# Attention scores: a mask added by two half-size products, and one reciprocal for two groups

## The chip, the cores and the metric

The kernel runs on one core of a Trainium2 chip. The metric is the device time of one execution in microseconds (us). Before the change the median of 3 runs is 858.65 us (858.62 to 858.83). The engines are PE (TensorE, matmuls; its weight loads are listed as PEld), DVE (VectorE), ACT (ScalarE), POOL (GpSimd) and SP, which issues the DMAs. Each engine runs its own instructions in program order and waits on semaphores for the others.

## What is computed

Attention with two kinds of heads, then two feed-forward blocks. 4 batches, 8 heads, 576 positions, 64 columns per head:

```python
scores = scale * np.matmul(q, k.transpose(0, 1, 3, 2))
rel = pos[:, None] - pos[None, :]
mask_local = (rel >= 0) & (rel < stride)                       # heads 0 to 3, stride = 32
mask_strided = (rel >= 0) & (pos[None, :] % stride == pos[:, None] % stride)   # heads 4 to 7
scores = np.where(masks[None, :, :, :], scores, -1000000000.0)
attn = np.exp(scores - max); attn = attn / (sum + 1e-09)
x = np.matmul(attn, v)            # 2304 rows of 512
h = x @ w_in; x = (h * np.cos(h)) @ w_out          # 512 -> 2048 -> 512
x = (silu(x @ w_gate) * (x @ w_val)) @ w_out2      # 512 -> 1536 -> 512
```

## The kernel before

The change lies in the attention stage, which takes about the first 100 us. The feed-forward stages follow it and fill the rest. All five engines' orders are those in which the code is written: there is no scheduler, and the pools only hand out buffers.

**Groups.** A unit is a pair of heads in one batch, its two heads on partitions 0 to 63 and 64 to 127. Units are strided and local in turn. Each unit is cut into 3 groups: a local group has 3 tiles of 64 queries by 96 keys, a strided one 4 tiles (the last of a unit 3) of 54 queries by 54 keys. The list `gs` holds 48 groups, strided and local alternating: even group numbers are strided, odd ones local.

**The loop.** One iteration `k` starts group `k` and carries older groups on (`LAGS` = 2, 5, 6, 7): `sums` of group k-2 (DVE: row sums, L490), `transposes` of group k-5 (PE, L501 local, L505 strided, into `tp`), `scores` of group k (PE, L466 to L469), `top` of group k (DVE: row maxima out of PSUM, L474; POOL: times the scale, L475, into `mx`), `put` of group k-7 (ACT: results to `xy`, L536, L545), `evac` of group k-5 (ACT: `tp` to `pt` or `pts`, L512), `values` of group k-6 (PE, L523, into `po`), `exps` of group k-1 (ACT, L481, bias `mx`), then `pump`, and last `norm` of group k-2 (DVE: reciprocal, L493; POOL: product, L495). So in an iteration's DVE order the reciprocal of group k-2 stands behind the pumped work, and in POOL's order the `mx` of a group and the product of an older one alternate.

**Pump.** From iteration 8 on, `pump(1.05)` takes about 1.05 us of DVE work out of a queue `fill`: the conversion of the w_in weights (ACT L254, DVE L257, L261, L265, the tile `wi`), scales (L126 to L145), the split of weights and inputs in a high and a low half (ACT L275, DVE L278), and the scan of w_out (L204). What a pump takes is fixed by the program.

**Scores.** For each tile of a group and each head, a product of 64 rows and 64 columns of the array (L466: head 0 on rows and columns 0 to 63, head 1 on 64 to 127), f32. Then a product of ones over columns 288 to 511 of the bank, whose result nobody reads (L468, bf16, the whole array), and then the identity times the mask over the whole array (L469, bf16), which adds the mask to the scores of both heads. All go to one PSUM bank: `start=True` is on the first score product.

After the 48 groups, 8 iterations drain the pipeline; in them PE does `keep_warm` products (L811) and the first tile of the feed-forward (`up1`, L581 to L583, with `up1_a`, ACT L614).

Of the kernel before, what the change touches and what calls it, by code (L numbers as in the profile page):

```python
# [10 lines left out]
F32 = mybir.dt.float32  # L11
# [39 lines left out]
LAGS = (2, 5, 6, 7)  # L51
# [30 lines left out]
def build(tc, qk_l, qk_s, v_l, v_s, w_in, w_out, w_gate, w_val, w_out2, fixed, out):  # L82
    nc = tc.nc
    wide = w_in.dtype != F32
    with ExitStack() as ctx:
# [12 lines left out]
        id16 = small.tile([128, 128], BF16, name="id16")  # L98
        ones16 = small.tile([128, 128], BF16, name="ones16")
# [75 lines left out]
        def release():  # L175
            if held_back[0]:
                held_back[0] -= 1
                next_raw()
            else:
                hold[0] = False  # L180
# [39 lines left out]
        def pump(share):  # L220

            credit[0] = min(credit[0] + share, max(share, 1.0))
            while fill and credit[0] > 0:
                step_fill()

        def need(key):
            while key not in emitted:
                step_fill()
# [99 lines left out]
        def direct_later(mat, j, tiles):  # L328
# [8 lines left out]
            rests.append((0.7, lambda: lo_part(tiles[j][:, 1], box["c"], scale_w[mat][0], tiles[j][:, 0]), (mat, j)))  # L337

        def seven_steps(j, stage, sums):

            boxes, conv = [], []
# [5 lines left out]
            def sources():  # L347
                f0, f1 = boxes[0]["c"], boxes[1]["c"]
                return ((stage[:, 0:1], f0[:, 0:256].rearrange("p (q n) -> p q n", q=1)),
                        (stage[:, 1:3], f1.rearrange("p (q n) -> p q n", q=2)), (stage[:, 3:7], sums))  # L350
# [54 lines left out]
        ap = attn.enter_context(tc.tile_pool(name="attn", bufs=2, side="right"))  # L405
# [8 lines left out]
        hot = ap.tile([128, 512], BF16, name="hot", bufs=1)  # L414
# [13 lines left out]
        def load_qk(i):  # L428
            b, p = units[i]
            loc = is_local(p)  # L430
            qk_t[i] = ap.tile([128, QKW[loc]], F32, name="qkl" if loc else "qks", bufs=3)
            nc.sync.dma_start(out=qk_t[i], in_=(qk_l if loc else qk_s)[b, p % 2])

        def load_v(i):
            b, p = units[i]
            loc = is_local(p)
            if loc:
                v_t[i] = ap.tile([128, LT, 128], F32, name="vl")
                nc.sync.dma_start(out=v_t[i], in_=v_l[b, p % 2])
            else:  # L440
                v_t[i] = v_pair[i // 2 % 2]
                for u in range(2):
                    nc.sync.dma_start(out=v_t[i][u:128:2, SP * u:SP * u + SP, :], in_=v_s[b, p % 2, u])

        def bank():
            return pm.tile([128, 512], F32, name="bank")

        class Group:
# [7 lines left out]
            def scores(self):  # L456
                n, w = self.n, self.w
                b = bank()
                self.sc = b[:, 0:n * w].rearrange("p (n w) -> p n w", w=w)
                mask = (ml[:, 0:3] if self.g == 0 else ml[:, 1:4]) if self.loc else ms[:, 0:n]  # L460
                for i in range(n):
                    q0 = (64 if self.loc else SW) * (self.i0 + i)
                    k0 = (S if self.loc else QP) + q0
                    for h in range(2):
                        r = slice(64 * h, 64 * h + 64)
                        nc.tensor.matmul(out=self.sc[r, i, :], lhsT=qk_t[self.i][r, q0:q0 + 64], rhs=qk_t[self.i][r, k0:k0 + w],  # L466
                                         start=i == 0, stop=False)
                nc.tensor.matmul(out=b[:, 288:512], lhsT=ones16, rhs=hot[:, 0:224], start=False, stop=False)  # L468
                nc.tensor.matmul(out=self.sc, lhsT=id16, rhs=mask, start=False, stop=True)  # L469

            def top(self):
                self.mx = ap.tile([128, 4], F32, name="mx", bufs=3)
# [7 lines left out]
                    e = self.t[:, i, 0:self.w] if self.loc else self.t[:, i // 2, 0:self.w, i % 2]  # L480
                    nc.scalar.activation(out=e, in_=self.sc[:, i, :], func=AF.Exp, scale=SCALE, bias=self.mx[:, i:i + 1])  # L481

            def sums(self):

                self.ls = ap.tile([128, 4], F32, name="ls", bufs=5)
                if self.loc:
                    self.l, self.e = self.ls[:, 0:3], self.t
                else:
                    self.l, self.e = self.ls.rearrange("p (a u) -> p a u", u=2), self.t.rearrange("p a k u -> p a u k")
                nc.vector.tensor_reduce(out=self.l, in_=self.e[..., 0:self.w + 1], op=ALU.add, axis=AX.X)  # L490

            def norm(self):
                nc.vector.reciprocal(out=self.l, in_=self.l)  # L493
                e = self.e[..., 0:self.w]
                nc.gpsimd.tensor_tensor(out=e, in0=e, in1=self.l.unsqueeze(len(e.shape) - 1).to_broadcast(list(e.shape)), op=ALU.mult)  # L495

# [104 lines left out]
        def up1(blk, m, ks=range(KC), c=None, spare=None):  # L601
            n = BLOCKS[blk][1]
            if m == 0 and not c:
                turn[blk] = prod(sx[blk][1], scale_w["in"][1], 1.0 / TWO_PI)
            if not c:
                b = bank() if spare is None else pacc.tile([128, 512], F32, name=f"acc{spare}")
                c = dict(n=n, ph=b[:, 0:n], blk=blk)
            project(c["ph"], wi[m], xs[blk], n, ks)
            return c

        def up1_a(c):
            n = c["n"]
            c["w"] = ring.tile([128, 512], F32, name="tb", bufs=4)[:, 0:n]
            nc.scalar.activation(out=c["w"].bitcast(I32), in_=c["ph"], func=AF.Identity, scale=turn[c["blk"]], bias=quarter)  # L614
# [194 lines left out]
        def keep_warm():  # L809
            t = bank()[:, 0:4 * LW].rearrange("p (n w) -> p n w", w=LW)  # L810
            nc.tensor.matmul(out=t, lhsT=id16, rhs=ml, start=True, stop=True)  # L811

        for k in range(len(gs) + LAGS[3] + 1):
            def group(lag):
                return gs[k - lag] if 0 <= k - lag < len(gs) else None
            i, g = 2 * (k // 6), k % 6
            if group(LAGS[0]):
                group(LAGS[0]).sums()
            if group(LAGS[1]):
                group(LAGS[1]).transposes()  # L820
            if group(0):
                group(0).scores()
                group(0).top()
            begun = k - len(gs) - K0
            if 0 <= begun < 2 * EARLY:
                m = begun // 2
                if begun % 2 == 0:
                    need(("in", m))
                    early = up1(0, m, range(KC // 2))
                else:  # L830
                    up1(0, m, range(KC // 2, KC), early)
                    up1_a(early)
                    steps.append((0, m, early))
            elif not group(0):
                keep_warm()
            if group(LAGS[3]):
                group(LAGS[3]).put()
            if group(LAGS[1]):
                group(LAGS[1]).evac()
            if group(LAGS[2]):  # L840
                group(LAGS[2]).values()
            if group(0) and g == 5:
                for j in (i + 2, i + 3):
                    if i and j < len(units):
                        load_v(j)
                for j in (i + 6, i + 7):
                    if j < len(units):
                        load_qk(j)
            if group(1):
                group(1).exps()  # L850
            pump(PUMP if k >= KP else 0)
            if group(LAGS[0]):
                group(LAGS[0]).norm()
            if k >= RELEASE:
                release()

# [344 lines left out]
        for s, (blk, j) in enumerate(slots):  # L1201
            n = BLOCKS[blk][1]
            h = n // 2
# [18 lines left out]
            def snap(src, h=h):  # L1222
                t = halves(ring.tile([128, 512], F32, name="cv", bufs=3), h)
                nc.scalar.activation(out=t, in_=src, func=AF.Copy)  # L1224
                return t
# [7 lines left out]
            a = begun or snap(px)  # L1233
# [7 lines left out]
            b = snap(pz)  # L1241
# [6 lines left out]
            a = snap(px)  # L1248
# [116 lines left out]
```

## Time and profile before

The profiled execution took 859.65 us; its span, first to last instruction, is 858.0 us.

| engine | busy us | share of span | instructions |
|---|---|---|---|
| PE | 844.9 | 98% | 7223 |
| PEld | 601.9 | 70% | 7223 |
| DVE | 653.6 | 76% | 1256 |
| ACT | 520.4 | 61% | 1047 |
| POOL | 200.0 | 23% | 281 |

How to read it: the shares are averages over stages with different limits, so a stage is read by the stretches of the table by windows. The granted TensorE clock is 1.00 of full speed throughout. A PE record's length contains the pipeline's latency, so what a PE instruction costs is the distance from its start to the next one's start. DVE and ACT records overlap their neighbours a little in the same way. In the chain that ended last, PE has 83%, DVE 11%.

### The profile page before, as it was taken

Reading aid. Unit: us, or ns where it says so; the run is one execution under the profiler, and the core shown is the slowest. Engines: PE = TensorE matmul, PEld = TensorE weight load, DVE = VectorE, ACT = ScalarE, POOL = GpSimd, SP = SyncE. Lnnn points to the kernel's source line nnn. Section 1 sums busy time; section 2 is a strip of 40 time slices with the busy share of each in tenths; the row PEclk is TensorE's granted clock in tenths of the full one; section 3 lists DMA queues with packets and bytes.
Section 4 is the critical chain, followed back from the end, with each engine's and each line's share of the span. In section 5 each row is a group of like instructions: output and inputs, shape, how many; then the busy total and the mean of one; then the engine's idle time right before and its main releaser. Section 6 shows DMA issues by size and latency. Waiting matters only on the chain.

```text
span 858.0 us, 18338 instructions
## 1 busy us (share of the span) xinstructions
PE 844.9 (98%) x7223; PEld 601.9 (70%) x7223; DVE 653.6 (76%) x1256; ACT 520.4 (61%) x1047; POOL 200.0 (23%) x281
## 2 busy tenths in 40 slices
PE   9999999999999999999999999999999999999998
PEld 5777544444444444555666788888888899999998
DVE  6999989997888978789996378567756765765562
ACT  6899889554657766768885466545344444444440
POOL 3454234211445546423223100000000000000000
PEclk9999999999999999999999999999999999999999
DMA  9998822897567566514356257667777688789894
GB/s 364 408 381 274 280 90 78 282 337 260 167 198 240 198 214 205 178 34 177 131 193 249 75 194 282 230 218 263 235 262 239 238 273 289 280 306 319 323 321 145
DMA packets 53605, 202.21 MB, mean 236 GB/s; under 512 B 5264, under 2 KB 15888, under 8 KB 49680
## 3 DMA queue, kind: packets, MB, share of 16 engines
q1 hardware_dynamic: 53520, 201.06, 67.3%
q8 instruction: 56, 0.92, 0.4%
q14 instruction: 29, 0.24, 0.1%
HBM read 177.05 MB, written 23.99 MB: 234 GB/s over the span
## 4 chain that ended last, share of the span: by engine, by line
PE 83%; DVE 11%; DMA 2%; ACT 2%; issue 1%; POOL 0%; SPq 0%; ACTq 0%; POOLq 0%
PE acc L734 14%; PE bank L581 13%; PE bank L582 12%; PE bank L583 12%; PE acc L583 7%; PE acc L581 7%; PE acc L582 7%; PE bank L466 3%; PE po L523 2%; DMA raw<-w_val 2%; DVE tb L624 1%; DVE tb L617 1%; PE tp L501 1%; DVE cv L265 1%; PE bank L468 1%
## 5 line engine op out<-in xcount | busy, mean ns | idle before, releaser
L581 PE MATMUL bank<-xs,wi 128*128 128x256 f16 (+3 forms) x776 | 231.1, 298 | 4.4 <-DVE q L145 1.7
L583 PE MATMUL bank<-xs,wi 128*128 128x256 f16 (+3 forms) x776 | 231.1, 298 | 0.0
L582 PE MATMUL bank<-xs,wi 128*128 128x256 f16 (+3 forms) x776 | 231.1, 298 | 0.0
L629 POOL TENSOR_TENSOR arena<-tb,arena 128x512 f16<-128x512 f32 (+1 forms) x80 | 91.5, 1144 | 239.6 <-ACT arena L628 212.9
L582 PEld LDWEIGHTS <-wi 128*128 128x128 f16 x880 | 86.1, 98 | 41.5 <-issue 7.2
L583 PE MATMUL acc<-arena 128*128 128x512 f16 (+1 forms) x320 | 114.5, 358 | 0.5 <-DVE arena L278 0.5
L581 PE MATMUL acc<-arena 128*128 128x512 f16 (+1 forms) x320 | 114.5, 358 | 0.0
L582 PE MATMUL acc<-arena 128*128 128x512 f16 (+1 forms) x320 | 114.5, 358 | 0.0
L581 PEld LDWEIGHTS <-wi 128*128 128x128 f16 x880 | 86.1, 98 | 36.0 <-issue 1.1
L583 PEld LDWEIGHTS <-wi 128*128 128x128 f16 x880 | 86.1, 98 | 34.7
L734 PEld LDWEIGHTS <-arena 128*128 128x128 f16 x1080 | 100.7, 98 | 8.1
L719 POOL TENSOR_TENSOR wi<-tb 128x256 f32<-128x256 f32 (+1 forms) x30 | 20.2, 675 | 338.5 <-DVE tb L701 338.5
L704 ACT ACTIVATE arena<-tb 128x256 f16<-128x256 f32 (+3 forms) x59 | 28.6, 485 | 99.0 <-DVE tb L701 90.6
L1228 DVE TENSOR_TENSOR arena<-bank,cv 128x512 f32<-128x512 f32 (+1 forms) x60 | 37.9, 636 | 66.0 <-PE bank L583 66.0
L583 PEld LDWEIGHTS <-arena 128*128 128x128 f16 x600 | 58.7, 98 | 33.7 <-DVE arena L278 1.0
L734 PE MATMUL acc<-arena 128*128 128x256 f16 (+1 forms) x702 | 82.0, 265 | 0.0
L582 PEld LDWEIGHTS <-arena 128*128 128x128 f16 x600 | 58.7, 98 | 32.6
L581 PEld LDWEIGHTS <-arena 128*128 128x128 f16 x600 | 58.7, 98 | 32.4
L628 ACT ACTIVATE arena<-tb 128x512 f16<-128x512 f32 (+1 forms) x80 | 46.6, 583 | 53.5 <-PE acc L583 51.9
L614 ACT ACTIVATE tb<-bank,quarter,c 128x512 int32<-128x512 f32 (+1 forms) x74 | 53.7, 725 | 33.7 <-PE bank L583 25.5
L701 DVE SCALAR_TENSOR_TENSOR tb<-tb,c,arena 128x512 f32<-128x512 f32 (+1 forms) x60 | 41.7, 695 | 35.8 <-ACT tb L696 35.8
L1224 ACT ACTIVATE cv<-bank 128x512 f32<-128x512 f32 (+1 forms) x90 | 49.3, 548 | 30.1 <-PE bank L583 29.1
(143 smaller groups left out, 1722.3 us busy)
## 6 DMA issues: line engine op xcount, KB each, us to landing
wi<-w SPq DMA_DIRECT2D x20, 1792.0 KB, 7.7
arena<-w SPq DMA_DIRECT2D x60, 576.0 KB, 4.9
raw<-w_out SPq DMA_DIRECT2D x56, 512.0 KB, 4.7
arena<-w SPq DMA_DIRECT2D x10, 1792.0 KB, 8.9
raw<-w_gate SPq DMA_DIRECT2D x24, 512.0 KB, 4.2
raw<-w_val SPq DMA_DIRECT2D x24, 512.0 KB, 5.6
w<-arena SPq DMA_DIRECT2D x42, 256.0 KB, 3.0
raw<-w_in SPq DMA_DIRECT2D x16, 512.0 KB, 9.1
```

The costliest lines, as they stand in the source:

```text
L466: nc.tensor.matmul(out=self.sc[r, i, :], lhsT=qk_t[self.i][r, q0:q0 + 64], rhs=qk_t[self.i][r, k0:k0 + w], start=i == 0, stop=False)
L581: nc.tensor.matmul(out=o, lhsT=w[:, 0, c], rhs=x[0], start=first, stop=False, **kw)
L582: nc.tensor.matmul(out=o, lhsT=w[:, 0, c], rhs=x[1], start=False, stop=False, **kw)
L583: nc.tensor.matmul(out=o, lhsT=w[:, 1, c], rhs=x[0], start=False, stop=last, **kw)
L614: nc.scalar.activation(out=c["w"].bitcast(I32), in_=c["ph"], func=AF.Identity, scale=turn[c["blk"]], bias=quarter)
L628: nc.scalar.activation(out=g[:, 0, 0:n], in_=w, func=AF.Copy)
L629: nc.gpsimd.tensor_tensor(out=g[:, 1, 0:n], in0=w, in1=g[:, 0, 0:n], op=ALU.subtract)
L701: nc.vector.scalar_tensor_tensor(out=t, in0=t, scalar=s_g[c["blk"]], in1=c["C"][m][:, 1, 0:c["n"]], op0=ALU.mult, op1=ALU.mult)
L704: nc.scalar.activation(out=to, in_=src, func=AF.Copy, scale=2.0 ** -11)
L734: nc.tensor.matmul(out=o[:, c], lhsT=w[:, 256 * i + 128 * c:256 * i + 128 * c + 128], rhs=unit(u)[:, x:x + h], start=j == c == i == 0, sto ...
L1224: nc.scalar.activation(out=t, in_=src, func=AF.Copy)
L1228: nc.vector.tensor_tensor(out=c["C"][m][:, :, h * right:h * right + h], in0=p, in1=t, op=ALU.add)
```

## The change

Three edits. First, the product of ones moves ahead of the score products and takes `start=True`. Second, the mask is added by two products of 64 rows and 64 columns, one a head, on the same quarters of the array as the scores. Third, the sums of a strided group and of the local group behind it go to one tile `ls` of 8 columns, and one reciprocal of 7 columns serves both: `sums` of the local group, then `invert`, then both `norm` products, all at the head of the local group's iteration; the strided group's norm thereby moves from the end of one iteration to the head of the next, the local group's from the end to the head of the same iteration.

```diff
@@ scores
                 mask = (ml[:, 0:3] if self.g == 0 else ml[:, 1:4]) if self.loc else ms[:, 0:n]
+                nc.tensor.matmul(out=b[:, 288:512], lhsT=ones16, rhs=hot[:, 0:224], start=True, stop=False)
                 for i in range(n):
...
                         nc.tensor.matmul(out=self.sc[r, i, :], lhsT=qk_t[self.i][r, q0:q0 + 64], rhs=qk_t[self.i][r, k0:k0 + w],
-                                         start=i == 0, stop=False)
-                nc.tensor.matmul(out=b[:, 288:512], lhsT=ones16, rhs=hot[:, 0:224], start=False, stop=False)
-                nc.tensor.matmul(out=self.sc, lhsT=id16, rhs=mask, start=False, stop=True)
+                                         start=False, stop=False)
+                for h in range(2):
+                    r = slice(64 * h, 64 * h + 64)
+                    nc.tensor.matmul(out=self.sc[r], lhsT=id16[r, r], rhs=mask[r], start=False, stop=True)
@@ sums, norm
-            def sums(self):
-                self.ls = ap.tile([128, 4], F32, name="ls", bufs=5)
+            def sums(self, mate):
                 if self.loc:
-                    self.l, self.e = self.ls[:, 0:3], self.t
+                    self.ls = mate.ls
+                    self.l, self.e = self.ls[:, 4:7], self.t
                 else:
...
+                    self.ls = ap.tile([128, 8], F32, name="ls", bufs=3)
+                    self.l = self.ls[:, 0:4].rearrange("p (a u) -> p a u", u=2)
...
+            def invert(self):
+                nc.vector.reciprocal(out=self.ls[:, 0:7], in_=self.ls[:, 0:7])
             def norm(self):
-                nc.vector.reciprocal(out=self.l, in_=self.l)
@@ the loop
             if group(LAGS[0]):
-                group(LAGS[0]).sums()
+                mate = group(LAGS[0] + 1)
+                group(LAGS[0]).sums(mate)
+                if group(LAGS[0]).loc:
+                    mate.invert()
+                    mate.norm()
+                    group(LAGS[0]).norm()
...
             pump(PUMP if k >= KP else 0)
-            if group(LAGS[0]):
-                group(LAGS[0]).norm()
```

On PE, one strided group before (`ones_77` are the weights of ones, `id_76` the identity, `fix` the mask's tile):

```order
L501 MATMUL tp<-fix,e_l_103 96x128 x3
L466 MATMUL bank<-qks 64x54 x8
L468 LDWEIGHTS ones_77
L468 MATMUL bank<-hot,ones_77 128x224
L469 LDWEIGHTS id_76
L469 MATMUL bank<-fix,id_76 128x216
L523 MATMUL po<-pts,v_pair_108 64x54 x8
```

and the same group now:

```order
L507 MATMUL tp<-fix,e_l_103 96x128 x3
L461 LDWEIGHTS ones_77
L461 MATMUL bank<-hot,ones_77 128x224
L467 MATMUL bank<-qks 64x54 x8
L471 LDWEIGHTS id_76
L471 MATMUL bank<-fix,id_76 64x216
L471 LDWEIGHTS id_76
L471 MATMUL bank<-fix,id_76 64x216
L529 MATMUL po<-pts,v_pair_108 64x54 x8
```

The whole-array product of ones now follows the whole-array transposes, and the mask follows the scores on the same quarters; a group has one matmul and one weight load more.

On POOL, where `e_s` and `e_l` are the exponentials of strided and local groups, a piece of the loop before:

```order
L495 TENSOR_TENSOR e_s_99<-e_s_99,ls 128x2x2x54
L475 TENSOR_SCALAR mx<-mx 128x3
L495 TENSOR_TENSOR e_l_103<-e_l_103,ls 128x3x96
L475 TENSOR_SCALAR mx<-mx 128x4
L495 TENSOR_TENSOR e_s_100<-e_s_100,ls 128x2x2x54
```

and the same piece now:

```order
L501 TENSOR_TENSOR e_s_99<-e_s_99,ls 128x2x2x54
L501 TENSOR_TENSOR e_l_103<-e_l_103,ls 128x3x96
L477 TENSOR_SCALAR mx<-mx 128x3
L477 TENSOR_SCALAR mx<-mx 128x4
L501 TENSOR_TENSOR e_s_100<-e_s_100,ls 128x2x2x54
```

The `mx` of each local group (the row with 3 columns) now stands behind two products, where it stood behind one that belonged to an older iteration. The orders of ACT and SP are unchanged.

## Rows read from the trace of the kernel before

**Rows 1.** Busy us by window: instruction counts, granted clock, DMA share, GB/s.

```profile
core 0: us, PE busy (x) PEld busy (x) DVE busy (x) ACT busy (x) POOL busy (x), PEclk, DMA share, GB/s
20.00:50.00 30.00, 30.00 (x507) 21.62 (x504) 28.82 (x78) 27.32 (x105) 15.14 (x32) 1.00 1.03 408
50.00:100.00 50.00, 49.54 (x794) 34.81 (x793) 47.32 (x134) 47.02 (x172) 23.34 (x49) 1.00 0.87 296
58.00:71.50 13.50, 13.50 (x235) 9.79 (x231) 12.49 (x37) 13.50 (x49) 7.31 (x15) 1.00 0.90 332
79.10:95.40 16.30, 16.23 (x247) 11.30 (x247) 15.62 (x41) 16.30 (x58) 7.87 (x16) 1.00 0.86 273
122.00:200.00 78.00, 76.90 (x358) 34.81 (x357) 76.81 (x135) 52.81 (x84) 21.12 (x19) 1.00 0.67 230
216.00:858.00 642.00, 634.15 (x5177) 483.14 (x5176) 459.74 (x825) 355.76 (x608) 125.05 (x137) 1.00 0.65 223
```

**Rows 2.** Timeline of PE, one strided group: start us, us, instruction, count.

```profile
38.72 0.53 PE L501 MATMUL tp<-fix,e_l 128*96 128x128 f32 x3
39.18 0.67 PE L466 MATMUL bank<-qks 64*64 64x54 f32 x16
39.79 0.27 PE L468 MATMUL bank<-hot,ones 128*128 128x224 bf16 x1
39.89 0.26 PE L469 MATMUL bank<-fix,id 128*128 128x216 bf16 x1
40.09 0.68 PE L523 MATMUL po<-pts,v_pair 108*64 108x54 f32 x16
40.69 0.44 PE L505 MATMUL tp<-fix,e_s 128*128 128x128 f32 x2
41.06 0.71 PE L466 MATMUL bank<-qkl 64*64 64x96 f32 x12
```

**Rows 3.** Timeline of PE, transposes ahead of a whole-array bf16 product.

```profile
90.89 0.53 PE L501 MATMUL tp<-fix,e_l 128*96 128x128 f32 x3
91.26 0.33 PE L811 MATMUL bank<-fix,id 128*128 128x384 bf16 x1
```

**Rows 4.** Groups of instructions, 0 to 225 us: busy us, mean ns, idle before.

```profile
L493 DVE RECIPROCAL ls<-ls 128x4 f32<-128x4 f32 (+1 forms) x48 | 8.0, 167 | 0.0
```

**Rows 5.** Timeline of DVE at two places: start us, us, instruction, idle before.

```profile
66.24 0.75 DVE L278 SCALAR_TENSOR_TENSOR xs<-xy,s,xs 128x512 f16<-128x512 f32 x1 [0.57 <-ACT xs L275]
...
76.36 0.17 DVE L493 RECIPROCAL ls<-ls 128x4 f32<-128x4 f32 x1
76.45 0.42 DVE L490 TENSOR_REDUCE ls<-e_l 128x3 f32<-128x291 f32 x1
76.79 0.45 DVE L474 TENSOR_REDUCE mx<-bank 128x3 f32<-128x288 f32 x1
```

**Rows 6.** Timeline of POOL, 76 to 79 us.

```profile
76.70 0.55 POOL L495 TENSOR_TENSOR e_s<-e_s,ls 128x216 f32<-128x216 f32 x1 [1.68 <-PE tp L501]
77.32 0.20 POOL L475 TENSOR_SCALAR mx<-mx 128x3 f32<-128x3 f32 x1
78.06 0.67 POOL L495 TENSOR_TENSOR e_l<-e_l,ls 128x288 f32<-128x288 f32 x1 [0.54 <-DVE ls L493]
78.69 0.20 POOL L475 TENSOR_SCALAR mx<-mx 128x3 f32<-128x3 f32 x1
```

**Rows 7.** Timeline of ACT at three places.

```profile
38.70 0.68 ACT L254 ACTIVATE wi<-raw 128x512 f32<-128x512 f32 x1 [1.98 <-DMA raw<-w_in]
...
77.56 0.81 ACT L481 ACTIVATE e_l<-bank,mx 128x96 f32<-128x96 f32 x3 [0.41 <-POOL mx L475]
79.03 1.33 ACT L275 ACTIVATE wi<-wi,s 128x512 f16<-128x512 f32 x2 [0.67 <-DVE s L120]
80.27 0.40 ACT L545 ACTIVATE xy<-po 128x96 f32<-128x96 f32 x2
80.49 0.39 ACT L512 ACTIVATE pts<-tp 128x256 f32<-128x256 f32 x1
...
96.15 0.78 ACT L614 ACTIVATE tb<-bank,quarter,c 128x512 int32<-128x512 f32 x1 [0.70 <-PE bank L583]
```

**Rows 8.** Timeline of PE at 81 us, the product that reads `pts`.

```profile
80.95 0.68 PE L523 MATMUL po<-pts,v_pair 108*64 108x54 f32 x16
```

More of the change, by code (lines that the diff above doesn't have):

```diff
@@ L481, in exps @@
                     nc.scalar.activation(out=e, in_=self.sc[:, i, :], func=AF.Exp, scale=SCALE, bias=self.mx[:, i:i + 1])
-            def sums(self):
-                self.ls = ap.tile([128, 4], F32, name="ls", bufs=5)
+            def sums(self, mate):
                 if self.loc:
-                    self.l, self.e = self.ls[:, 0:3], self.t
-                else:
-                    self.l, self.e = self.ls.rearrange("p (a u) -> p a u", u=2), self.t.rearrange("p a k u -> p a u k")
+                    self.ls = mate.ls
+                    self.l, self.e = self.ls[:, 4:7], self.t
+                else:
+                    self.ls = ap.tile([128, 8], F32, name="ls", bufs=3)
+                    self.l = self.ls[:, 0:4].rearrange("p (a u) -> p a u", u=2)
+                    self.e = self.t.rearrange("p a k u -> p a u k")
                 nc.vector.tensor_reduce(out=self.l, in_=self.e[..., 0:self.w + 1], op=ALU.add, axis=AX.X)
+            def invert(self):
+                nc.vector.reciprocal(out=self.ls[:, 0:7], in_=self.ls[:, 0:7])
             def norm(self):
-                nc.vector.reciprocal(out=self.l, in_=self.l)
                 e = self.e[..., 0:self.w]
```

## The prediction

> **What bounds the kernel now.** I read the busy time by window first. From 216 us to the end PE is busy 634.15 of 642 us: whatever ends earlier before that, the end moves with it. From 122 to 200 us DVE is full (76.81 of 78), but its work is started by the attention stage's end and nothing there hangs on a clock of its own, so a shift passes through that too. What has to be known is how far the attention stage's end, at about 101 us, moves. There three engines stand close together: from 50 to 100 us PE is busy 49.54, DVE 47.32, ACT 47.02 of 50 us, and ACT is full from 58 to 71.5 and from 79.1 to 95.4 [rows 1].
>
> Then the timelines. PE goes through its groups without a stall, about 1.9 us each (39.18 to 41.06 is 1.88) [rows 2], so the stage looks bound by PE. But its partners follow closely. At 80.49 ACT moves `pts` out, done at 80.88, and PE starts on it at 80.95 [rows 7, 8]: 0.07 us of room. The DMA engines are full from 20 to 50 us (share 1.03) and ACT waits 1.98 us for a piece of w_in that lands at 38.70 [rows 1, 7]; that landing does not move when PE is faster. So the stage is paced by PE, with ACT less than 0.1 us behind it at some places.
>
> **PE.** What one change between whole-array and quarter-array products costs can be read: three transposes take 0.46 us up to the first quarter product (38.72 to 39.18) and 0.37 us up to a whole-array product (90.89 to 91.26), so 0.09 us [rows 2, 3]. The mask, 216 columns, takes 0.20 us up to the next form of product, the ones, 224 columns, 0.10 us up to the mask that has their own form: 0.10 us again [rows 2]. Before, a group has four such changes (into the scores, out to the ones, into the values, out to the transposes); now the ones follow the transposes and the mask the scores, and three are left. If the two mask halves run beside each other, as long as one, a group gets 0.09 us shorter: 48 x 0.09 = 4.3 us of PE. Do they? No row shows two bf16 halves. The nearest is the score block: 16 passes of 54 columns go from 39.18 to 39.79, 0.52 us without the change of form; at the transposes' pace (0.37 / 3 for 128 columns, 0.052 for 54) they would take 0.83 us one after the other [rows 2, 3]. So halves of this kind overlap, into one bank, and I take 0. Serial, they would add the columns once more, about 0.10 us. Between -0.09 and +0.01 a group I take -0.09. The extra weight load stands behind score passes and is costed at nothing; if it isn't covered, it eats at most the gain.
>
> The Trainium skill, TensorEngine Tiling (Array Packing), Restrictions and Gotchas, says the opposite of the overlap: different row tiles cannot access the same PSUM bank simultaneously. By that rule the halves would be serial and PE's sum would be +0.5 us instead of -4.3; the score rows speak against it here, where the halves write different partitions, and it stays as a rival below.
>
> **DVE.** 24 of 48 reciprocals go (those left have 7 columns instead of 3 or 4). From one's start to the next start is 0.09 us (76.36 to 76.45) [rows 5], so 24 x 0.09 = 2.2 us; the records' own 167 ns [rows 4] would be 4.0, which is the bound. Nothing else on DVE changes in number.
>
> **POOL, and what stands behind it.** The same 48 products and 48 `mx`, in another order. This is the added wait: `mx` of a local group is queued behind both products, which wait for the reciprocal. Take the group at 76 to 78 us. Sums start at 76.45, and 0.34 us later DVE is free for the reciprocal, 76.79. Reciprocal to product takes 0.34 (76.36 to 76.70), the strided product up to the next POOL start 0.62 (76.70 to 77.32), the local one 0.63 (78.06 to 78.69): `mx` starts at 76.79 + 0.34 + 0.62 + 0.63 = 78.38 instead of 77.32, 1.06 us later [rows 5, 6]. Behind it on ACT wait that group's exps, which now start 0.04 us after `mx` ends (77.52 to 77.56) [rows 6, 7], and behind them all of ACT. For the strided groups `mx` has nothing new ahead of it.
>
> **What of this reaches the end.** Up to 38.70 all gain is lost to the landing of w_in, since PE has next to no room ahead of ACT just after it. From 50 us on DVE frees about 0.09 us each 3.8 us, but at 66.24 it already waits 0.57 us for ACT [rows 5], which is full from 58 to 71.5: gains before that are lost there, and about 3 pairs are left to 77 us, 0.3 us. At 77.56 the exps start 1.06 - 0.3 = 0.8 us later; ACT's own idle there (0.67 before 79.03) takes most of it, since they take 0.81 us and ended at about 78.4: now about 79.2, so L275 starts some 0.2 us late, and the `pts` of 80.49 too. PE, which could be 2 to 3 us ahead by then, starts its product at about 81.1, not before 80.95. From there 8 groups to 96 us save PE 8 x 0.09 = 0.7; ACT, full from 79.1 to 95.4, arrives at 95.4 + 0.2 plus a further late `mx` or two, for which I take 0.2 (nothing to 1.06), and has 0.70 us of idle before 96.15 to give. So ACT's next step starts at about 95.9 instead of 96.15: a gain of about 0.25 us of the 4.3 that PE saves.
>
> The profiled execution (859.65: span 858.0 and 1.65 around it) would thus take 859.4; the median of the runs shown lies 1.0 lower, so 858.4 us.
>
> **Rivals.** (1) The late `mx` is hidden and PE's gain comes through. For it: DVE has fewer instructions ahead of the sums, so everything could slide together. Against it: ACT has no work less, and from 50 to 100 us it idles only 2.98 us [rows 1], which is the most that the stage can shrink there without ACT losing anything, whatever PE saves; ACT's waits for DVE and `mx` won't go to zero. Between 0.25 and 2.98 I take 2.6: 856.0 us.
> (2) Slower: the late `mx` closes a loop. `mx` (0.20), exps (0.04 + 0.81), sums (0.34), reciprocal to product (0.34), two products (0.62 + 0.63) and `mx` again add to 2.98 us, against 3.76 for two groups on PE [rows 2, 5 to 7]. In that time ACT also has to do one `evac` and one `put` ahead of the exps (80.27 to 80.88, 0.61) and a pumped step (0.68) [rows 7]: 4.27 if these fall behind `mx`, 0.5 over PE's pace. It decides from the point where exps wait for `mx` in most local groups with ACT's work queued behind them rather than done before. From 50 to 96 us are 12 pairs: 12 x 0.5 = 6.0 at most; half of them, less the idle already there at 96.15 (0.70), 2.3: 861.0 us. Against it: the earlier work on ACT needs no `mx` and can be done while it waits.
> (3) The mask halves are serial: PE +0.01 a group, 48 x 0.01 = +0.5, and the partners' room stays: 859.2 us.
>
> **How the numbers follow.** Forecast 0.55, rival 1 0.20, rival 2 0.17, rival 3 0.08. About 0.2%, 1.7 us, is what can be told from no change. The forecast's own range is 857.2 to 859.6. Faster than 856.9: rival 1 and a little of the forecast, 0.22; slower than 860.4: rival 2 and a little, 0.19; within, 0.59. The range reaches to rival 1's middle and rival 2's: 855.9 to 860.9.
>
> **What would show it.** Right: PE's group drops from 1.88 to about 1.79 us where it doesn't wait; the mask halves start some 0.01 us apart; exps of local groups wait for `mx` on ACT far more than 0.41 us, at 77 us above all; PE waits for ACT's `pts` or `pt` or for POOL's product where it waited for nothing; the stage's last ACT step (L614) starts within 0.5 us of 96.15. Wrong on PE: mask halves 0.1 us apart (rival 3). Wrong on the partners: L614 at 94 us or earlier (rival 1), or at 98 (rival 2).

## The result, and the profile after

The changed kernel takes 864.12 us (median of 4 runs, 863.71 to 864.64) against 858.74 us (858.62 to 858.85) for the kernel before: a ratio of 1.0057, 95% interval 1.0045 to 1.007. It is slower by 5.4 us; 858.4 was forecast. The profiled execution took 863.71 us with a span of 861.9, at full clock.

The profiled executions lie 4.06 us apart, less than the medians, since that of the kernel before (859.65) is 0.9 over its median and that of the changed one 0.4 under.

The loss is there when the attention stage ends. The timeline of PE gives the first product behind the stage, in the kernel before (L581) and after (L587):

```profile
101.09 0.38 PE L581 MATMUL acc<-xs,wi 128*128 128x512 f16 x1 [0.50 <-ACT xy L536]
```

```profile
105.85 0.38 PE L587 MATMUL acc<-xs,wi 128*128 128x512 f16 x1 [0.50 <-ACT xy L542]
```

The stage ends 4.76 us later. Behind it 0.7 us of that is made up: PE of the kernel before waits 0.54 us for DVE at 204.60 us, the changed one does not, and at PE's next wait for DVE, at 207.74 us before and 211.79 after, the distance is 4.05. The prediction's own mark, L614 at 96.15 us [rows 7], is L620 on ACT's timeline now, 4.75 us late:

```profile
100.90 0.78 ACT L620 ACTIVATE tb<-bank,quarter,c 128x512 int32<-128x512 f32 x1
```

**PE became faster, as predicted.** Timeline of PE before, the scores of the local group that stands ahead of [rows 2]:

```profile
37.25 0.71 PE L466 MATMUL bank<-qkl 64*64 64x96 f32 x12
```

and after, the same place:

```profile
37.66 0.26 PE L461 MATMUL bank<-hot,ones 128*128 128x224 bf16 x1
...
39.12 0.53 PE L507 MATMUL tp<-fix,e_l 128*96 128x128 f32 x3
39.48 0.26 PE L461 MATMUL bank<-hot,ones 128*128 128x224 bf16 x1
39.67 0.67 PE L467 MATMUL bank<-qks 64*64 64x54 f32 x16
40.18 0.26 PE L471 MATMUL bank<-fix,id 64*64 64x216 bf16 x2
40.43 0.68 PE L529 MATMUL po<-pts,v_pair 108*64 108x54 f32 x16
41.39 0.44 PE L511 MATMUL tp<-fix,e_s 128*128 128x128 f32 x2 [0.29 <-POOL e_s L501]
```

Both strided mask halves (x2) together take 0.26 us, as the one whole-array mask did [rows 2], so they run beside each other. The local group from 37.66 to 39.48 takes 1.82 us, where before it took 1.93, from its scores at 37.25 to the next group's at 39.18 [rows 2]; a strided group of 4 tiles that doesn't wait (60.26 to 62.03) takes 1.77 instead of 1.88. But at 41.39 PE waits for POOL, and it never waited there before.

**PE no longer sets the pace.** The same windows as in [rows 1], after:

```profile
20.00:50.00 30.00, 26.84 (x485) 20.02 (x482) 29.55 (x69) 26.60 (x104) 15.27 (x30) 1.00 1.02 403
50.00:100.00 50.00, 45.53 (x781) 33.40 (x780) 46.91 (x118) 43.10 (x163) 23.68 (x50) 1.00 0.76 272
```

From 20 to 50 us PE fell from 30.00 to 26.84 and DVE rose from 28.82 to 29.55, which is full. DVE has 24 instructions fewer in the stage (215 instead of 239 from 6 us to its end) and is busy longer: 89.25 us instead of 85.64. So its instructions got longer. Groups by line and shape, 18 to 106 us (busy us, mean ns, idle before), first of the kernel before:

```profile
L265 DVE SCALAR_TENSOR_TENSOR wi<-raw,wi 128x512 int32<-128x512 int32 x16 | 11.2, 701 | 0.3
L257 DVE TENSOR_REDUCE pw_in<-raw 128x1 f32<-128x512 f32 x16 | 10.8, 676 | 0.0
L495 POOL TENSOR_TENSOR e_l<-e_l,ls 128x288 f32<-128x288 f32 x21 | 14.0, 668 | 17.6 <-DVE ls L493 11.9 <-ACT xy L536 2.3 <-ACT pt L512 1.5
```

and of the changed one:

```profile
L265 DVE SCALAR_TENSOR_TENSOR wi<-raw,wi 128x512 int32<-128x512 int32 x16 | 13.4, 834 | 0.3
L257 DVE TENSOR_REDUCE pw_in<-raw 128x1 f32<-128x512 f32 x16 | 10.8, 674 | 0.0
L501 POOL TENSOR_TENSOR e_l<-e_l,ls 128x288 f32<-128x288 f32 x21 | 17.7, 843 | 0.0
```

L265, which reads two tiles, went from 701 to 834 ns, and POOL's product, which also reads two, from 668 to 843. L257, a reduction of one tile, did not change. The timelines of DVE and then of POOL, after, show how these meet:

```profile
27.70 0.44 DVE L494 TENSOR_REDUCE ls<-e_l 128x3 f32<-128x291 f32 x1
28.18 0.20 DVE L497 RECIPROCAL ls<-ls 128x7 f32<-128x7 f32 x1
28.29 0.42 DVE L476 TENSOR_REDUCE mx<-bank 128x3 f32<-128x288 f32 x1
28.70 0.68 DVE L261 TENSOR_SCALAR wi<-wi 128x512 int32<-128x512 int32 x1
29.42 1.04 DVE L265 SCALAR_TENSOR_TENSOR wi<-raw,wi 128x512 int32<-128x512 int32 x1
30.38 0.37 DVE L494 TENSOR_REDUCE ls<-e_s 128x4 f32<-128x220 f32 x1
...
31.55 0.41 DVE L261 TENSOR_SCALAR wi<-wi 128x512 int32<-128x512 int32 x1
...
35.32 0.69 DVE L265 SCALAR_TENSOR_TENSOR wi<-raw,wi 128x512 int32<-128x512 int32 x1
```

```profile
28.55 0.55 POOL L501 TENSOR_TENSOR e_s<-e_s,ls 128x216 f32<-128x216 f32 x1 [1.31 <-DVE ls L497]
29.06 0.85 POOL L501 TENSOR_TENSOR e_l<-e_l,ls 128x288 f32<-128x288 f32 x1
29.88 0.63 POOL L477 TENSOR_SCALAR mx<-mx 128x3 f32<-128x3 f32 x1
...
36.79 0.55 POOL L501 TENSOR_TENSOR e_s<-e_s,ls 128x216 f32<-128x216 f32 x1 [1.45 <-DVE ls L497]
```

The L265 that starts while a product runs (29.42, inside 29.06 to 29.91) takes 1.04 us; the one at 35.32, with no product beside it, 0.69. Seven of the 16 L265 now start with over 0.4 us of a product left and take 1.01 to 1.04 us. In the old order the products began behind a reciprocal at the end of an iteration and ran mostly beside the next iteration's sums and maxima; one L265 was slowed there, to 0.89. Now both begin behind `invert` at the head of a local iteration and run beside the conversion steps that are pumped in that iteration.

The count of inputs does not tell it all. L261 reads one tile only: free of products it takes 0.41 us (31.55), and 0.68 at 28.70, inside the product of 28.55. Five of 16 are slowed, to 0.68 to 0.79; before, five were, to 0.62 to 0.68. And POOL is held too: the local product that starts at 29.06, inside that L261, takes 0.85, and the `mx` at 29.88, inside L265, 0.63 instead of 0.20 [rows 6].

The same rows show a second price. The sums start at 27.70 and the reciprocal, which reads them, at 28.18: 0.48 us. Before, the instruction behind the sums read something else and started 0.34 us behind them [rows 5]. A sum over all of DVE's timeline rows from 6 us to the stage's end, each from its start to the next start with the listed idle time taken off:

| DVE time in the stage, us | before | after |
|---|---|---|
| conversion with two inputs (L265 and L278 on `wi`), x27 | 18.07 | 20.93 |
| L261, x16 | 7.68 | 8.23 |
| sums of local groups, x24 | 8.75 | 11.58 |
| sums of strided groups, x24 | 7.20 | 6.98 |
| reciprocals | 4.79 (x48) | 2.84 (x24) |

The 24 reciprocals saved are 1.95 us; the wait for the sums just ahead of the one that is left costs 2.83. The conversion (the first two rows) costs 3.41 more, and strided sums 0.22 less. Together that is 4.07 us of DVE's time, beside the 4.76 by which the stage ends later. That it all lies on the path to that end is not shown.

Third, waits in the stage (8 to 106 us: total, times, longest), before:

```profile
ACT e_l L481 <- POOL mx L475: 0.8, 3, 0.4
```

and after, ACT's and PE's longest:

```profile
ACT e_l L483 <- POOL mx L477: 12.4, 18, 1.3
```

```profile
PE tp L511 <- POOL e_s L501: 4.9, 13, 0.7
```

### The profile page after: what moved, and what is told of

Same layout as the page of the kernel before. It is cut to its first block, busy times and chain, and to the rows that moved or that the text cites. A ratio compares the mean times of both kernels' runs of the same rounds, so it can differ in the third digit from the quotient of the medians.

```text
span 861.9 us, 18369 instructions
## 1 busy us (share of the span) xinstructions
PE 841.4 (98%) x7271; PEld 601.8 (70%) x7271; DVE 656.0 (76%) x1232; ACT 519.2 (60%) x1047; POOL 202.6 (24%) x281
## 4 chain that ended last, share of the span: by engine, by line
PE 82%; DVE 10%; ACT 4%; POOL 2%; issue 1%; POOLq 0%; ACTq 0%; DVEq 0%
PE acc L740 14%; PE bank L587 13%; PE bank L589 13%; PE bank L588 13%; PE acc L587 9%; PE acc L589 9%; PE acc L588 9%; DVE ls L494 1%; DVE mx L476 1%; ACT e_l L483 1%; DVE xs L278 1%; POOL e_s L501 1%; DVE tb L623 1%; DVE tb L630 1%; POOL e_l L501 1%
## 5 line engine op out<-in xcount | busy, mean ns | idle before, releaser
L587 PE MATMUL bank<-xs,wi 128*128 128x256 f16 (+3 forms) x776 | 231.1, 298 | 4.4 <-DVE q L145 1.7
L587 PE MATMUL acc<-arena 128*128 128x512 f16 (+1 forms) x320 | 114.5, 358 | 0.0
L587 PEld LDWEIGHTS <-wi 128*128 128x128 f16 x880 | 86.1, 98 | 36.1 <-issue 1.1
L587 PEld LDWEIGHTS <-arena 128*128 128x128 f16 x600 | 58.7, 98 | 32.5
L620 ACT ACTIVATE tb<-bank,quarter,c 128x512 int32<-128x512 f32 (+1 forms) x74 | 53.7, 725 | 33.8 <-PE bank L589 26.1
```

What stands on the lines that cost most here:

```text
L587: nc.tensor.matmul(out=o, lhsT=w[:, 0, c], rhs=x[0], start=first, stop=False, **kw)
```

## The experiments

Three theories stood against each other. T1: POOL's products now lie beside DVE's pumped steps, and both engines get slower. T2: `mx` of a local group stands behind two products, and the exps on ACT wait. T3: the strided product comes too late for PE's transposes. Differences below are to the kernel before in the same set of runs (858.74 to 859.29).

**The two halves of the change apart.** The first run keeps the shared reciprocal and the moved products, with the old score products:

```diff
-                nc.tensor.matmul(out=b[:, 288:512], lhsT=ones16, rhs=hot[:, 0:224], start=True, stop=False)
...
-                for h in range(2):
-                    r = slice(64 * h, 64 * h + 64)
-                    nc.tensor.matmul(out=self.sc[r], lhsT=id16[r, r], rhs=mask[r], start=False, stop=True)
+                nc.tensor.matmul(out=b[:, 288:512], lhsT=ones16, rhs=hot[:, 0:224], start=False, stop=False)
+                nc.tensor.matmul(out=self.sc, lhsT=id16, rhs=mask, start=False, stop=True)
```

> The changed kernel with the score products of before (whole-array mask, ones behind the scores); shared reciprocal and early products stay. All three theories that blame the move of POOL's products (T1: the two products run beside pumped DVE instructions and both slow down; T2: mx of the local groups is queued behind them; T3: the strided group's product comes too late for its transposes) expect the loss here in full, 863 to 866 us, PE's groups at 1.87 to 1.93 us where they don't wait. Rival: the loss comes from the mask halves; then 858 to 859.

Measured: 864.46 us, 5.4 over before, ratio 1.0061 [1.0046, 1.0076]. L265 has a mean of 832 ns, and ACT waits 12.3 us for `mx`. The whole loss comes with the reciprocal's half.

The second run is the kernel before with only the new score products (the reverse of that edit):

> The kernel before with the new score products alone. T1 to T3: no loss; PE's groups 0.10 us shorter, of which little comes through since DVE and ACT are nearly full: 856.5 to 858.5 us. Rival (mask halves): 862 to 864.

Measured: a median of 858.95 us of 10 runs that spread from 858.45 to 864.84, ratio 1.0009 [0.9993, 1.0025]: no gain, where 856.5 to 858.5 was expected. The profiled one took 861.79. Its timeline of PE, and then that of ACT:

```profile
37.75 0.26 PE L471 MATMUL bank<-fix,id 64*64 64x216 bf16 x2
40.08 1.11 PE L525 MATMUL po<-pts,v_pair 108*64 108x54 f32 x16 [2.07 <-ACT pts L514]
```

```profile
38.73 0.67 ACT L254 ACTIVATE wi<-raw 128x512 f32<-128x512 f32 x1 [2.93 <-DMA raw<-w_in]
39.31 0.51 ACT L547 ACTIVATE xy<-po 128x168 f32<-128x168 f32 x2
39.63 0.40 ACT L514 ACTIVATE pts<-tp 128x256 f32<-128x256 f32 x1
```

The piece of w_in lands at 38.73; it was 38.70 before [rows 7]. PE is ahead by then and stands for 2.07 us. What follows, by windows (the granted clock is the figure behind POOL's count):

```profile
40.00:42.00 2.00, 1.92 (x21) 1.43 (x23) 1.15 (x3) 2.00 (x11) 0.53 (x2) 0.50 1.03 408
48.00:50.00 2.00, 2.00 (x27) 1.52 (x25) 0.80 (x3) 1.23 (x5) 0.63 (x2) 0.51 1.04 401
52.00:60.00 8.00, 8.00 (x145) 5.99 (x144) 7.86 (x23) 7.51 (x31) 3.42 (x9) 1.00 0.61 240
```

After that stall PE had half clock, 1.2 GHz, up to 50 us. So the score products' gain ends at the landing, and the stall there can cost more.

**T3: the products later.** The changed kernel, with `invert` and both products behind the pumped steps:

```diff
             if group(LAGS[0]):
                 mate = group(LAGS[0] + 1)
                 group(LAGS[0]).sums(mate)
-                if group(LAGS[0]).loc:
-                    mate.invert()
-                    mate.norm()
-                    group(LAGS[0]).norm()
...
             pump(PUMP if k >= KP else 0)
+            if group(LAGS[0]) and group(LAGS[0]).loc:
+                mate.invert()
+                mate.norm()
+                group(LAGS[0]).norm()
```

> The changed kernel with reciprocal and both products moved behind the pumped work of the local group's iteration, so they run beside the next iteration's sums and maxima, and mx of the local group is ahead of them. T1: DVE L265 back to about 0.70 us, POOL's local product to 0.67, 857 to 859.5 us. T2: waits of ACT for mx of local groups gone, those of strided groups perhaps up, 858 to 860. T3: the strided product comes a pump (about 1.2 us) later still, so PE waits more: 865 us or above.

Measured: 865.42 us, 6.4 over before. ACT's waits for `mx` of local groups fell to 1.0 us (those for strided ones rose from 1.2 to 3.3), but PE's waits for the strided product doubled, from 4.9 to 9.8 us. L265 still had 786 ns and POOL's product 823: the products met the next iteration's steps. T1's number was missed, since its cause was not taken away; with the `mx` early, PE waits for the strided product instead, as T3 said.

**T2: `mx` first.** The changed kernel, with both products queued behind `mx`:

```diff
                 if group(LAGS[0]).loc:
                     mate.invert()
-                    mate.norm()
-                    group(LAGS[0]).norm()
...
+            if group(LAGS[0]) and group(LAGS[0]).loc:
+                mate.norm()
+                group(LAGS[0]).norm()
```

> The changed kernel with the shared reciprocal at its place, but both products queued on POOL behind mx of the local group. T2: the loss is mostly gone, 858 to 860 us, ACT's waits for mx under 4 us in all. T1: the products still run beside the pumped DVE work, L265 stays near 0.83, 862 us or above. T3: the strided product is later by about 0.3 us, 864 or above.

Measured: 862.25 us, 3.2 over before, ratio 1.0036 [1.0023, 1.0049]. ACT's waits for `mx` of local groups fell from 12.4 to 2.4 us. That is 2.2 us of the 5.4, less than T2 expected. They are not all the late `mx`: the products moved too, and L265 had 786 ns here instead of 834, POOL's local product 795 instead of 843.

**T3 again: one iteration more of room.** The changed kernel, with the transposes and all that follows one iteration later:

```diff
-LAGS = (2, 5, 6, 7)
+LAGS = (2, 6, 7, 8)
```

> The changed kernel with LAGS = (2, 6, 7, 8): transposes and all behind them one iteration later, so the strided product has some 1.8 us more. T3 (it comes too late for its transposes): PE's waits for POOL's e_s (4.9 us in the changed kernel, 2.6 with the old score products) vanish and some 3 us of the loss with them, 860 to 861.5 us, with about 0.8 us for one more iteration of the drain in it. T2 alone (late mx): no less than 863. T1 alone (DVE slowed by POOL): no less than 863.

Measured: 868.62 us, 9.7 over before. PE's waits for the strided product went from 4.9 us to none worth a row, and the stage ended later all the same, at 107.41 instead of 105.85; the waits stand at the values now (6.0 us for `pt`). So PE's wait for POOL was not a cause by itself. Part of the loss lies behind the stage: at 369.84 us PE has waited 2.98 us for DVE, where the changed kernel waits 0.71, and its granted clock is 0.64 from 370 to 374 us. Why DVE is late there stays open.

**T1: the two-input step replaced.** L265 of the w_in conversion is replaced by a reduction that reads one tile, in the changed kernel and in the one before; both thus leave out the last step of that conversion, w_in's low bits:

```diff
+                if mat == "in":
+                    nc.vector.tensor_reduce(out=dummy, in_=box["h"].bitcast(F32), op=ALU.max, axis=AX.X, apply_absolute_value=True)
+                    free()
+                    return
```

> The changed kernel, in which the w_in conversion leaves out its last step (L265, two SBUF inputs) and runs a reduction of one input over the high words in its place; to be held against the next run. T1: the slowing of L265 (701 to 834 ns, 16 times, 2.1 us) is gone, so this kernel is at most 3.5 us above e7. T2 and T3: the distance stays 5 us or more.

> The kernel before with the same step left out and replaced. All theories: within 1.5 us of the kernel before, the base for the run above.

Measured: the changed one 860.84 us (860.34 to 861.02, 10 runs), the one before 859.04 (858.4 to 859.57, 10 runs). The kernel before does not care (ratio 0.9998 [0.9989, 1.0008]), since its 701 ns become 675. The gap between the two falls from 5.4 to 1.8 us, so 3.6 us hang on L265 beside the products. That is more than L265's own 2.1 us (16 times 133 ns). Groups of the changed one with this edit:

```profile
L267 DVE TENSOR_REDUCE dummy<-raw 128x1 f32<-128x512 f32 x16 | 10.8, 675 | 0.0
L506 POOL TENSOR_TENSOR e_l<-e_l,ls 128x288 f32<-128x288 f32 x22 | 16.5, 752 | 0.0
```

POOL's product gets shorter too (843 to 752 ns), though nothing of POOL was changed, and ACT's waits for `mx` of local groups fall from 12.4 to 9.3 us. So part of T2's loss goes with T1's.

**T1 and T2 together.** `mx` first, and L265 replaced in the same way:

```diff
                 if group(LAGS[0]).loc:
                     mate.invert()
-                    mate.norm()
-                    group(LAGS[0]).norm()
...
+            if group(LAGS[0]) and group(LAGS[0]).loc:
+                mate.norm()
+                group(LAGS[0]).norm()
...
+                if mat == "in":
+                    nc.vector.tensor_reduce(out=dummy, in_=box["h"].bitcast(F32), op=ALU.max, axis=AX.X, apply_absolute_value=True)
```

> Both products queued behind mx of the local group, and the w_in conversion's last step left out and replaced by a reduction of one input, as in e6. If DVE slowed by POOL (T1) and the late mx (T2) are the loss together, 858.5 to 860 us against 859.04 of e7; if the late strided product (T3) has a part of its own that shows only when the others are gone, 860.5 to 862 with PE waiting for e_s.

Measured: 859.71 us, ratio 1.0005 [0.9996, 1.0015]; 0.7 over the kernel before with the same replacement. PE still waits 4.3 us for the strided product. With T1's step and T2's order taken away, 0.7 of the 5.4 us are left.

**T1 in the kernel before.** Its own reciprocals stay two, but each comes right behind its sums, and each product right behind that iteration's `mx`:

```diff
             def sums(self):
...
+                nc.vector.reciprocal(out=self.l, in_=self.l)
             def norm(self):
-                nc.vector.reciprocal(out=self.l, in_=self.l)
...
+            if group(LAGS[0]):
+                group(LAGS[0]).norm()
...
             pump(PUMP if k >= KP else 0)
-            if group(LAGS[0]):
-                group(LAGS[0]).norm()
```

> The kernel before, with 48 reciprocals and the old score products, but each group's reciprocal right behind its sums and its POOL product right behind the mx of that iteration: no shared reciprocal, no late strided product, no mx behind two products; only the product now runs beside the pumped DVE work instead of the next iteration's sums. T1: L265 at 0.78 to 0.85 us instead of 0.70 and a slower kernel, 860.5 to 863 us, though every product is earlier than before. If place beside the pumped work is harmless (the loss needs the pairing of two products): 858.3 to 859.3, L265 near 0.70.

Measured: 871.36 us (866.02 to 874.75, 4 runs), ratio 1.0154 [1.0131, 1.0178]. The mean granted clock was 0.984 to 0.992 in the three higher runs and 0.998 in the lowest, the profiled one, which alone is read here: 6.7 over before, more than expected. In it too PE waited 2.01 us for DVE ahead of 61.48 us and had a clock of 0.50 from 63 to 66. Its timelines of DVE and POOL:

```profile
28.86 1.20 DVE L265 SCALAR_TENSOR_TENSOR wi<-raw,wi 128x512 int32<-128x512 int32 x1
...
32.77 0.68 DVE L265 SCALAR_TENSOR_TENSOR wi<-raw,wi 128x512 int32<-128x512 int32 x1
```

```profile
28.85 0.66 POOL L495 TENSOR_TENSOR e_l<-e_l,ls 128x288 f32<-128x288 f32 x1
...
33.48 0.66 POOL L495 TENSOR_TENSOR e_l<-e_l,ls 128x288 f32<-128x288 f32 x1
```

At 28.85 the product starts first and keeps its 0.66 us; L265 starts 0.01 us behind it and takes 1.20 instead of 0.68. That is T1 in a kernel without the change: nine of its 16 L265 take 1.07 to 1.20. ACT waits 10.5 us for `mx` here, though no product of its iteration stands ahead of it; POOL itself waits 50.6 us for DVE's maxima. So a wait for `mx` is not by itself a sign of T2. The run holds a second price as well, which its expectation did not count: two reciprocals that wait for their sums. In the table above its conversion would stand at 21.25 us, its sums at 11.57 (local) and 9.78 (strided), 5.4 us over before. How its loss divides between the two and the half clock isn't settled.

**Where the gain of the scores went.** First, only the new score products with one iteration more between scores and values:

```diff
-LAGS = (2, 5, 6, 7)
+LAGS = (2, 5, 7, 8)
```

> The kernel before with the new score products and LAGS = (2, 5, 7, 8): values and put one iteration later, so PE may lead ACT by some 1.8 us more. If PE's lead is lost to the landing of w_in at 38.7 us (a stall of 2.07 us there in the scores-only kernel, and the granted clock falling to 0.5 behind it), the stall is gone, the clock stays at 1.00 and the time is 857 to 858.7 us without runs above 860. If DVE and ACT are the limit anyway, the time is that of the kernel before plus the longer drain, 859 to 860.

Measured: 862.74 us, 3.9 over before, above both forecasts. PE still stands from about 38.2 to 40.42 us, for 2.23 us, only for another tile (`xy`), since ACT sits at the same landing, now at 39.43. More room behind the landing does not help. Only 1.0 us of the loss is there at the stage's end (102.12 us); later PE waits 2.98 us for DVE ahead of 364.54, where the kernel before waits 0.71. The clock stayed at 1.00 here, so a stall of this length does not always lower it.

Then the landing itself: q and k of later units are loaded later, so that w_in's pieces come earlier, with the new score products and, as a control, in the kernel before:

```diff
-                for j in (i + 6, i + 7):
+            if group(0) and g == 2 and i:
+                for j in (i + 4, i + 5):
                     if j < len(units):
                         load_qk(j)
```

> The kernel before with the new score products, and q and k of later units loaded three iterations later, so that two pieces of w_in stand ahead of them in the DMA queue. If the landing of w_in at 38.7 us is the wall that takes PE's gain, it moves to about 36 us, PE's stall and the fall of the clock there go, and the time is 855.5 to 857.5 us. If DVE and ACT are the limit without the wall: 858 to 859. A loss would come from q and k landing too late.

> The kernel before with the later loads alone. PE sets its pace, so an earlier landing of w_in gives little: 857.5 to 858.9 us. If it alone gives all that e10 gives, the score products add nothing.

Measured: 857.21 us (856.99 to 857.78, 11 runs), ratio 0.9979 [0.9971, 0.9988], against 858.75 (ratio 0.9995 [0.9986, 1.0004]) for the control. The slowest run of the first lies below the fastest of the control (858.53). ACT takes that piece of w_in at 36.21 us, without a wait. Its timeline of PE, at the place of the stall and at the stage's end:

```profile
38.33 0.26 PE L471 MATMUL bank<-fix,id 64*64 64x216 bf16 x2
38.52 0.68 PE L525 MATMUL po<-pts,v_pair 108*64 108x54 f32 x16
39.12 0.44 PE L507 MATMUL tp<-fix,e_s 128*128 128x128 f32 x2
...
99.81 0.38 PE L583 MATMUL acc<-xs,wi 128*128 128x512 f16 x1 [0.50 <-ACT xy L538]
```

No stall, and the stage ends at 99.81 instead of 101.09 us. Of the 4.3 us forecast for PE the score products bring 1.5 (858.75 to 857.21) once the landing is out of the way; the earlier landing alone brings nothing clear.

## Why the prediction was wrong

**PE: right.** Groups that don't wait got 0.10 to 0.11 us shorter (1.88 to 1.77, 1.93 to 1.82), where 0.09 was forecast, and the mask halves overlap. The Trainium skill, TensorEngine Tiling (Array Packing), Restrictions and Gotchas, has row tiles unable to use one PSUM bank at the same time; the trace differs here, with two halves in 0.26 us, and the measurement decides. Rival 3 falls with it.

**The landing at 38.70: right in its mechanism.** The run with the scores alone and the one with later q and k loads show both sides of it. In the changed kernel itself it didn't come to bear: ACT reached that piece at 39.02 us, without a wait. Not foreseen was that a stall there can cost more than the gain, by way of the clock.

**DVE: the step that failed.** "24 x 0.09 = 2.2 us" were to go, and "nothing else on DVE changes in number". In number, nothing did. But the step took each duration as fixed, from a trace in which one L265 of 16 was slowed, and moved the products onto the pumped steps, where seven were. The conversion took 3.41 us more, and the runs put 3.6 us of the loss on the meeting of L265 and the products. POOL's sum has the same fault: it takes 0.63 us for the local product, which now has a mean record of 843 ns instead of 668. A row that spoke of it was in the trace before. Timelines of DVE and POOL of the kernel before:

```profile
36.89 0.89 DVE L265 SCALAR_TENSOR_TENSOR wi<-raw,wi 128x512 int32<-128x512 int32 x1
```

```profile
36.57 0.67 POOL L495 TENSOR_TENSOR e_l<-e_l,ls 128x288 f32<-128x288 f32 x1 [0.87 <-DVE ls L493]
```

This L265 started inside a product and took 0.89 us, where its neighbours took 0.69. The prediction read POOL's order and DVE's order each for itself, and never laid the products' new places over DVE's rows.

The Trainium skill, SBUF — State Buffer, SBUF: two separate sides, says it outright: DVE and GpSimd share a pair of ports under an exclusive lock, which a DVE instruction takes in a mode that uses two ports, or with two SBUF inputs against a GpSimd one that reads SBUF, and the later one waits in full. This case's traces agree in kind: at 28.85 us in the run with early products the first kept its 0.66 us, and L265 took 0.52 more. The rule would have it wait for the rest of the product, some 0.65 us by that row. L261, with one input, was held as well; in which mode it ran no run here shows.

The saved 2.2 us were wrong as well: by the table 1.95 go and 2.83 come back in the local sums, since a reciprocal that reads the sums just ahead of it waits for them. The prediction took the distance from one start to the next from rows where neighbours did not depend on each other. This is read from rows; no run isolates it. In the run with the products last, whose reciprocal stands behind the pumped steps, the local sums have 9.89 us by the same count, against 11.58.

**POOL: `mx` late, right in place and short in size.** The exps wait up to 1.3 us for it. The sum gave that 0.2 us and one or two more late `mx`; in fact the exps of 18 local groups wait, 12.4 us in all. Putting `mx` first gives 2.2 us back, some of it by way of T1. Rival 2 had this mechanism and the sign, at 861.0 us. It lacked T1.

**The stage's end:** L614 was to come within 0.5 us of 96.15 and came at 100.90; of the marks named for "wrong on the partners", 98 and more was the one that showed.

What stays open: T1 (3.6 us) and T2 (2.2) add to 5.8 where 5.4 were lost and 0.7 are left with both mended. They overlap, and the share of the dependent reciprocal and of PE's wait for POOL in the remainder is not told apart.

## What to carry to other kernels

When instructions of one engine move, lay their new places over the other engines' rows and ask what they will run beside: a duration from the trace holds only for the neighbours that it had there, and single rows that stick out of a group's mean (0.89 among 0.69) show the price ahead of time. Before counting a merged instruction as saved, look whether it now stands right behind what it reads. And a faster engine that only runs sooner into a fixed landing gains nothing until that landing moves: move the loads first, then speed up the engine.

## What the runs showed of the hardware

- A DVE instruction of 128x512 with two inputs (L265) took 0.67 to 0.69 us alone and 0.89 to 1.20 us when it started inside a POOL product with 0.35 to 0.65 us of it left. A one-input one (L261) took 0.41 to 0.43 alone and 0.62 to 0.79 with 0.34 to 0.50 left. A reduction of one tile (L257) kept a mean of 674 to 677 ns in every run.
- It holds POOL in the same way: a POOL step of 128x3 took 0.20 us alone and 0.63 when it started inside an L265.
- A reciprocal right behind the reduction that it reads started 0.48 us after that reduction's start (changed kernel, 27.70 and 28.18), where an independent instruction started after 0.34 (kernel before, 76.45 and 76.79).
- After a stall of 2.07 us PE had a granted clock of 0.50 (1.2 GHz) for the 10 us up to 50 us, though it was busy throughout (the run with the scores alone); after one of 2.23 us in another kernel it kept 1.00.
